# Experts with up to 232 tokens by four plain products, shorter switches on VectorE and ScalarE, and earlier gathers

## The chip, the cores and the metric

The kernel runs on one core of a Trainium2 chip. The metric is the device time of one launch in microseconds (us). Runs of one kernel differ by some tenths of a per cent.

## The reference, cut to what matters

A chunked attention (4 batches, 8 heads, 768 positions, heads of 64) makes 3072 rows of 512 numbers. A router then gives each row to one of eight experts, and each expert is a network of two layers without biases. All numbers are float32.

```python
logits = x @ w_gate                       # x: (3072, 512)
expert_idx = np.argmax(logits, axis=1)
...
for e in range(E):                        # E = 8, F = 1024
    lo, hi = (boundaries[e], boundaries[e + 1])
    h = np.maximum(x_sorted[lo:hi] @ w1[e], 0.0)     # w1[e]: (512, 1024)
    y_sorted[lo:hi] = h @ w2[e]                      # w2[e]: (1024, 512)
y = y_sorted[inv_perm]
return (gate_w[:, None] * y).astype(np.float32)
```

The inputs are random with a fixed seed. With them the eight experts receive 529, 195, 426, 381, 565, 320, 162 and 494 rows.

## The kernel before

**Attention and routing** fill the first 190 us or so. Each finished block of 96 rows is scattered to `x_dram` in the order of its experts. Of expert 0, 256 early rows are already done there by ordinary products (`early_rows`), so that 273 remain. `count_up` then counts the rows of each expert on VectorE, and works out `cases` (which variant of TensorE's code an expert takes) and `rows` (which rows of `x_dram` a gather fetches).

**The expert stage** is one critical section, written out by hand. `op` records a step: its engine, a function that emits it, and the tiles that it reads and writes. From these it works out the semaphore waits. The steps are collected in `plan`, and at the end `emit` writes them engine by engine; the order of recording is thus the order on each engine's queue, and nothing reorders it.

For each expert there is first an *interlude* (`interlude`): TensorE transposes the five gathered groups of 128 rows (`turn_x`; ScalarE copies groups 0, 2, 4 and VectorE 1, 3 into `xsT`), and then the five groups of the last expert's result (`turn_y`; VectorE scales group 1 into `y`, ScalarE the others). These transposes rotate over four halves of two PSUM tiles: `sum_x` (X) and `sum_q` (Q). VectorE also makes the first two differences T of the expert's rows.

Then comes the expert itself (`expert`), which is three calls of `layer`: the two halves of the first layer (k = 2 blocks of 128 in each quarter) and the last layer (k = 4). A call treats its matrix product as 2 x 2 quarters and does it by **seven products instead of eight**, with sums and differences of quarters (S of the weights, T of the rows), as in Strassen's method in Winograd's form. The expert's rows are split in two halves of up to 320 columns each, and the products work on one half's width. In the order of `layer` the products and what follows them on the other engines are:

1. P, then `over`: ScalarE copies P to R.
2. Q, then a snapshot of Q to a tile `kept`.
3. P again (added on top), then a snapshot of P.
4. R, then `evict(0, 0)`: ScalarE writes a quarter of the result.
5. P again, `over` once more, then `finish(1, 1)`: VectorE adds P and the first snapshot into a quarter of the result.
6. Q again, then `lift(1, 1)` (ScalarE's relu in the first layer) and `finish(0, 1)` on VectorE.
7. R again, then `lift(0, 1)` and `evict(1, 0)`.

The lists `at` place VectorE's sums S and T between these steps (`more(1)` to `more(7)`); among them are the sums S for the next expert's first layer, done during this expert's last layer. In the list the last of them stood at place 7, ahead of `finish(0, 1)`.

How many columns the products have is only known when the kernel runs. TensorE's code for an expert is therefore built in 24 **arms** (`ARMS`), one for each width of 136, 144 ... 320. A `Switch` on `cases` picks the arm; three products before an arm's end a hint is issued for the next expert's. VectorE and ScalarE have no switch: they always work on all 320 columns of a half.

```python
ARMS = list(range(136, HALF + 1, 8))
...
for a in nc.Switch(engines=[nc.tensor], index=[index[e]], n=len(ARMS), hint=f"expert{e}"):
    for i, s in enumerate(arm):
        if i == len(arm) - 3 and e + 1 < E:
            hint(e + 1)
        emit(s, ARMS[a])
```

**The queue of POOL** carries the stores of the results (`put`) and the gathers of the next expert's rows (`get_x`). Both are put in a list `sends`, and `tick` issues one of them after every second product of the first layer and after every product of the last; `pace` makes it wait until TensorE is there. `get_x` was called between the first layer and the last: a memset that marks all places of the row buffer as empty, and five gathers. The queue of SP carries the weights (`get_w`), after the first layer and after the last.

Of the kernel before, what the change touches and what calls it, by code (L numbers as in the profile page):

```python
# [73 lines left out]
ARMS = list(range(136, HALF + 1, 8))  # L74
# [430 lines left out]
def ordinary(ctx, tc, q, k, v, mem_k, mem_v, moe_w_gate, moe_w1, moe_w2, out, good):  # L505
# [352 lines left out]
    cases = cpool.tile([128, E], I32, name="cases")  # L858
    n0 = cpool.tile([128, 1], F32, name="n0")
# [34 lines left out]
    def count_up():  # L894
# [15 lines left out]
        nc.vector.tensor_copy(each, c)  # L910
        nc.vector.tensor_scalar(c, c, 7, None, op0=OP.add)
        nc.vector.tensor_scalar(c, c, 3, None, op0=OP.arith_shift_right)
        nc.vector.tensor_scalar(c, c, ARMS[0] // 8, HALF // 8, op0=OP.max, op1=OP.min)
        nc.vector.tensor_scalar(c, c, ARMS[0] // 8, None, op0=OP.subtract)
# [258 lines left out]
    def op(eng, fn, reads=(), writes=(), dma=None, where="after", pace=False):  # L1173
        need = {}

        def after(stamp):
            sem, n = stamp
            if not sem == eng == "PE" and known[eng].get(sem, 0) < n:
                need[sem] = max(need.get(sem, 0), n)

        if pace:
            after(("PE", counts["PE"]))
        for x in reads:
            if x in wrote:
                after(wrote[x])
        for x in writes:
            if x in wrote:
                after(wrote[x])
            for stamp in read.get(x, {}).items():
                after(stamp)  # L1190
        for sem, n in list(need.items()):
            if known[eng].get(sem, 0) >= n:
                continue
            for s, m in list(past.get((sem, n), {}).items()) + [(sem, n)]:
                known[eng][s] = max(known[eng].get(s, 0), m)
        sem, by = (dma, 16) if dma else (eng, 1)
        counts[sem] = counts.get(sem, 0) + by
        stamp = (sem, counts[sem])
        past[stamp] = dict(known[eng])
        for x in writes:  # L1200
            wrote[x] = stamp
            read[x] = {}
        for x in reads:
            read.setdefault(x, {})[sem] = counts[sem]
        plan.append((eng, fn, sorted(need.items()), (sem, by), where))

    def emit(step, n=None):
        eng, fn, need, (sem, by), _ = step
        first = []
# [75 lines left out]
    def get_x(e):  # L1285
# [3 lines left out]
        op("POOL", one_op(lambda: nc.gpsimd.memset(x[:, :, DM].bitcast(I32), SKIP)), [], [("xe", e % 2)])  # L1289
        for g in range(NG):  # L1290
# [11 lines left out]
            sends.append(lambda pace, g=g, fn=fn: batch(f"get{e % 2}", "POOL", fn, ("xe", e % 2), g == 0))  # L1302
# [54 lines left out]
    def product(to, names, A, B, reads, first, last, e, ms=(0, 1)):  # L1357
        k = A.shape[1]

        def fn(n):  # L1360
            made = []
            for m in ms:
                for i in range(k):
                    made.append(
                        mm(
                            to[:, m, 0:n],
                            lhsT=A[:, i, 128 * m : 128 * m + 128],
                            rhs=B[:, i, 0:n],
                            start=first and i == 0,
                            stop=last and i == k - 1,  # L1370
                            skip_group_check=True,
                        )
                    )
            return made[0], made[-1]
# [9 lines left out]
    def layer(e, A, a_names, S, s_names, B, b_names, T, t_names, C, c_names, relu, soon, at):  # L1384
# [17 lines left out]
        def evict(m, y, of, names):  # L1402
            op("ACT", one_op(lambda: nc.scalar.activation(C[m][y], of[:, :, 0:HALF], func)), [], names + [c_names[m][y]])
# [14 lines left out]
        product(P, p, A[0][0], B[0][0], [w] + b_names[0][0], True, False, e)  # L1418
# [4 lines left out]
        product(Q, q, S[0], T[0], [s_names[0], t_names[0]], True, False, e)  # L1423
        snapshot("M5", Q, q)
        more(5)
        product(P, p, S[1], T[1], [s_names[1], t_names[1]], False, False, e)
        snapshot("U2", P, p)
        more(6)
        product(R, r, A[0][1], B[1][0], [w] + b_names[1][0], False, True, e)
        evict(0, 0, R, r)  # L1430
        more(2)
        product(P, p, A[1][0], B[0][1], [a21] + b_names[0][1], False, True, e)
# [3 lines left out]
        product(Q, q, S[2], B[1][1], [s_names[2]] + b_names[1][1], False, True, e)  # L1436
# [14 lines left out]
        evict(1, 0, R, r)  # L1451
# [36 lines left out]
    def expert(e):  # L1488
        A1, A2 = quarters(e, 0), quarters(e, 1)
# [10 lines left out]
        for a in range(2):  # L1500
# [7 lines left out]
            layer(e, part, w1n, [x[:, :, a] for x in S1], s1n, B1, b1, T1, t1n, hs, hn, True, a == 1, at)  # L1508
        if e + 2 < E:
            get_w(e + 2, 0)  # L1510
        assert not sends
        if e < E - 1:
            get_x(e + 1)
            tick()
# [3 lines left out]
        at = {1: [t2[1]], 5: [t2[2], s2[3], s2[2]], 6: [t2[3]] + more[0:1], 2: more[1:2], 7: more[2:3]}  # L1518
        layer(e, A2, w2n, S2, s2n, B2, b2, T2, t2n, ys, yn, False, True, at)
# [6 lines left out]
    for e in range(E):  # L1526
# [3 lines left out]
        sums2[e] = weight_sums(e, 1, ["DVE"] * 4)  # L1530
    for g in range(2):
# [12 lines left out]
    with tc.tile_critical(no_gpsimd_drain=True):  # L1544
        for e in range(E + 1):
# [7 lines left out]
            for a in nc.Switch(engines=[nc.tensor], index=[index[e]], n=len(ARMS), hint=f"expert{e}"):  # L1553
                for i, s in enumerate(arm):
                    if i == len(arm) - 3 and e + 1 < E:
                        hint(e + 1)
                    emit(s, ARMS[a])
        for s in plan:
            if s[4] == "after":
                emit(s)  # L1560
# [50 lines left out]
```

## Time and profile before

| | |
|---|---|
| median of 3 runs | 538.32 us (535.3 to 539.24) |
| profiled execution | 532.34 us |
| its span, first to last instruction | 530.6 us |
| TensorE busy (PE) | 507.7 us, 96% of the span |
| TensorE's weight loads (PEld) | 475.7 us |
| VectorE (DVE) | 300.0 us, 57% |
| ScalarE (ACT) | 245.7 us, 46% |
| GpSimd (POOL) | 156.0 us, 29% |
| mean granted clock of TensorE | 0.994 |
| first transposes of expert 0 | at 190.46 us |
| first product of experts 1 to 7 | at 227.01, 258.49, 304.06, 345.14, 404.16, 439.32, 470.81 us |

The profile is of one execution, and all its times count from the first instruction. Busy time is the time in which an engine executes; an engine's sequencer, which handles loads of registers, jumps and hints, has rows of its own with a q (ACTq, DVEq, PEldq, POOLq, SPq). Lines such as L511 are those of the kernel before; L511 is the helper that every matmul goes through, L516 that of transposes, L1224 that of VectorE's sums, and L1227 that of ScalarE's copies `over` and `snapshot`, so groups are told apart by their tiles.

### The profile page before, as it was taken

To read this page: it belongs to the slowest core of one execution; us is meant where nothing else is said; L and a number is where in the kernel's file an instruction comes from. 1 tells how busy PE (TensorE), PEld (TensorE's weight loads), DVE (VectorE), ACT (ScalarE), POOL (GpSimd) and SP (SyncE) were. 2 spreads that over 40 slices of the span, in tenths; PEclk is the share of its full clock that TensorE was granted. 3 is DMA by queue.
4 is the path that set the end of the run, shared out by engine and by line. 5 is a ranking of instruction groups with operands and counts; after the bars stand their busy time and mean duration, and the time that the engine had idled before them with its cause. 6 is when DMAs were issued, how large, how long until landed. Compare 5 with 4: busy or idle time off the path is not lost.

```text
span 530.6 us, 9604 instructions
## 1 busy us (share of the span) xinstructions
PE 507.7 (96%) x3666; PEld 475.7 (90%) x3666; DVE 300.0 (57%) x565; ACT 245.7 (46%) x445; POOL 156.0 (29%) x186
## 2 busy tenths in 40 slices
PE   3999999999999989999999999999999999999992
PEld 3899999999998569999999999977779999999991
DVE  3455656566555246878656557443625767864611
ACT  2466656556632136374553454344216637454311
POOL 2000131323373604354135054121312434412003
PEclk9999999999999999999999999999999999999997
DMA  9999999989982302446406335330505334200002
GB/s 171 154 171 181 182 224 200 224 201 344 303 308 73 88 15 81 172 172 229 176 15 221 96 128 208 102 134 30 195 18 199 139 125 182 81 15 13 1 1 84
DMA packets 81350, 75.02 MB, mean 141 GB/s; under 512 B 39543, under 2 KB 64375, under 8 KB 81281
## 3 DMA queue, kind: packets, MB, share of 16 engines
q1 hardware_dynamic: 71840, 54.60, 41.6%
q0 software_dynamic: 8768, 19.29, 11.0%
q8 instruction: 46, 0.75, 0.6%
q10 hardware_dynamic: 672, 0.18, 0.1%
q14 instruction: 24, 0.19, 0.1%
HBM read 66.13 MB, written 17.50 MB: 158 GB/s over the span
## 4 chain that ended last, share of the span: by engine, by line
PE 83%; issue 9%; DMA 3%; POOL 2%; ACT 1%; DVE 1%; POOLq 0%; ACTq 0%
PE sum_p L511 20%; PE sum_r L511 13%; PE sum_q L511 13%; PE o L511 11%; PE sc L511 8%; PE tqk L516 4%; PE sum_x L516 3%; PE ph L511 3%; PE py L511 3%; PE sum_q L516 2%; PE tx L516 2%; POOL out_dram L1276 2%; DMA xe<-x_dram,rows 1%; DMA x_dram<-xr,dest 1%; DMA kn<-in_k_dram 1%
## 5 line engine op out<-in xcount | busy, mean ns | idle before, releaser
L1276 POOL DMA_INDIRECT out_dram<-y,xe x42 | 51.0, 1214 | 177.1 <-PE sum_q L511 59.9
L1293 POOL DMA_INDIRECT xe<-x_dram,rows x35 | 50.7, 1448 | 49.8 <-PE sum_r L511 29.2
L676 ACT ACTIVATE ex<-sc,cst 128x256 f32<-128x256 f32 x96 | 38.5, 472 | 56.5 <-PE sc L511 56.5
L511 PE MATMUL o<-v,ex 128*96 128x65 f32 x512 | 54.5, 251 | 0.0
L1227 ACT COPY sum_r<-sum_p 128x640 f32<-128x640 f32 x48 | 32.5, 677 | 47.3 <-PE sum_p L511 47.2
L511 PE MATMUL sc<-qT,kT 128*128 128x192 f32 x256 | 50.6, 343 | 1.1 <-ACT qT L627 1.1
L511 PEld LDWEIGHTS o<-v,ex 128*96 128x96 f32 x512 | 49.4, 167 | 0.0
L511 PE MATMUL sum_p<-xsT,w 128*128 128x136 f32 (+6 forms) x256 | 47.6, 329 | 0.5
L511 PE MATMUL sum_r<-t,w 128*128 128x136 f32 (+6 forms) x256 | 45.8, 326 | 0.0
L511 PE MATMUL sum_p<-t,s 128*128 128x136 f32 (+6 forms) x256 | 45.6, 326 | 0.0
L801 POOL DMA_INDIRECT x_dram<-xr,dest x32 | 30.2, 944 | 52.5 <-PE tqk L516 21.3
L511 PE MATMUL sum_q<-t,s 128*128 128x136 f32 (+6 forms) x256 | 45.1, 324 | 0.0
L511 PEld LDWEIGHTS sc<-qT,kT 128*128 128x128 f32 x256 | 43.2, 199 | 1.4 <-issue 1.4
L511 PEld LDWEIGHTS sum_p<-xsT,w 128*128 128x128 f32 x256 | 39.7, 190 | 4.8 <-issue 2.1
L511 PE MATMUL sum_p<-h,w 128*128 128x136 f32 (+6 forms) x256 | 43.8, 324 | 0.0
L511 PEld LDWEIGHTS sum_p<-t,s 128*128 128x128 f32 x256 | 39.7, 190 | 2.6
L511 PEld LDWEIGHTS sum_r<-t,w 128*128 128x128 f32 x256 | 39.6, 190 | 2.6
L511 PEld LDWEIGHTS sum_q<-t,s 128*128 128x128 f32 x256 | 39.8, 190 | 2.3
L511 PEld LDWEIGHTS sum_p<-h,w 128*128 128x128 f32 x256 | 39.5, 190 | 2.3
L1224 DVE TENSOR_TENSOR h<-sum_p,kept 128x640 f32<-128x640 f32 x16 | 13.2, 824 | 48.4 <-ACT sum_r L1227 48.4
L645 DVE COPY kT<-tqk 64x384 f32<-64x384 f32 x62 | 34.3, 554 | 10.4 <-PE tqk L516 9.8
L690 DVE RECIPROCAL inv_all<-o 96x4 f32<-96x4 f32 x64 | 11.4, 179 | 48.0 <-PE o L511 47.7
(154 smaller groups left out, 916.9 us busy)
## 6 DMA issues: line engine op xcount, KB each, us to landing
w<-in_moe_w_dram SPq DMA_DIRECT2D x14, 2048.0 KB, 8.6
kn<-in_k_dram SPq DMA_DIRECT2D x16, 384.0 KB
qn<-in_q_dram SPq DMA_DIRECT2D x16, 384.0 KB
w<-in_moe_w_dram SPq DMA_DIRECT2D x8, 512.0 KB
v<-in_v_dram SPq DMA_DIRECT2D x24, 128.0 KB
v<-in_v_dram SPq DMA_DIRECT2D x24, 112.0 KB
v<-in_v_dram SPq DMA_DIRECT2D x8, 144.0 KB
v<-in_v_dram SPq DMA_DIRECT2D x8, 96.0 KB
```

The lines of the kernel that those rows point to most:

```text
L511: i = nc.tensor.matmul(*args, **more)
L516: i = nc.tensor.transpose(*args)
L645: i = copy(to, of[:, :, 0:PAIRS].rearrange("d a (y z p) -> d a y z p", y=2, z=2))
L676: nc.scalar.activation(ex4[:, :, :, sl], sc4[:, :, :, sl], AF.Exp, bias=mask[:, 3 * x + g : 3 * x + g + 1], scale=D**-0.5)
L690: nc.vector.reciprocal(inv, o[:, :, D])
L801: i = nc.gpsimd.indirect_dma_start(out=x_dram, out_offset=bass.IndirectOffsetOnAxis(ap=dest[:, t : t + 1], axis=0), in_=xr[:, t % NXR].bit ...
L1224: op(eng, one_op(lambda: engines[eng].tensor_tensor(out, a, b, op=how)), reads, writes)
L1227: op("ACT", one_op(lambda: nc.scalar.copy(to, of)), reads, writes)
L1276: return nc.gpsimd.indirect_dma_start(out=out, out_offset=bass.IndirectOffsetOnAxis(ap=which.bitcast(I32), axis=0), in_=y, in_offset=None, ...
L1293: return nc.gpsimd.indirect_dma_start(out=x[:, g].bitcast(I32), out_offset=None, in_=x_dram, in_offset=bass.IndirectOffsetOnAxis(ap=rows[: ...
```

## The change

It has three parts.

- **A second way through an expert.** Thirteen arms are added (136 to 232 columns, marked True). They are taken where an expert has at most `FEW` = 232 rows. `count_up` then puts all rows in one half. In these arms a call of `layer` does the four plain products of its quarters: the first two product steps do one half of the lower quarter each into F (the tile P or Q), the step R does both upper products, and one of the steps 5 and 6 does the second lower product. The other steps, three in each call, are a single one-column matmul that keeps the semaphore counts (`nothing`). In the last layer, two matmuls of the R step cover 320 columns.
- **Switches on VectorE and ScalarE.** From an expert's start until a point in its last layer, each of their steps exists twice: as before, and as `few`, where it is a copy of one column (`skip`), or for `evict` a copy from the tile that now has the result. A `Switch` on `fews` picks one. ScalarE leaves it after the second snapshot of the last layer, VectorE after the last of that layer's T sums. The value is loaded and the hint given four steps before the next switch.
- **Gathers.** `get_x` for the next expert is called before the second half of the first layer rather than after the first layer; its memset is issued with the first gather.

Two smaller edits: the sum S that stood at place 7 of the last layer now stands at place 3, after `finish(0, 1)`; and two tiles `kept` are set to zero at the start of the critical section.

```diff
-ARMS = list(range(136, HALF + 1, 8))
+FEW = 232
+ARMS = [(n, False) for n in range(136, HALF + 1, 8)] + [(n, True) for n in range(136, FEW + 1, 8)]
...
         nc.vector.tensor_copy(each, c)
+        nc.vector.tensor_scalar(few, count, float(FEW), None, op0=OP.is_le)
+        nc.vector.tensor_tensor(more, count, each, op=OP.subtract)
+        nc.vector.tensor_tensor(more, more, few, op=OP.mult)
+        nc.vector.tensor_tensor(each, each, more, op=OP.add)
+        nc.vector.tensor_copy(c, each)
+        nc.vector.tensor_scalar(fews, count, float(FEW), None, op0=OP.is_le)
...
+    def skip(eng):
+        spot[0] = (spot[0] + 1) % 32
+        to = spots[eng][:, spot[0] : spot[0] + 1]
+        return one_op(lambda: skips[eng](to, cst[:, 0:1]))
+
+    inside = dict(DVE=None, ACT=None)
+
+    def op(eng, fn, reads=(), writes=(), dma=None, where="after", pace=False, few=None):
         need = {}
+        if inside.get(eng) is not None:
+            where = ("inside", inside[eng])
+            fn.few = few or skip(eng)
...
+        nothing = one_op(lambda: mm(unread, lhsT=ident[:, 0:1], rhs=ident[:, 0:1], start=False, stop=True, skip_group_check=True))
+        fn.few = of(few) if few else nothing
...
+        low0 = [[(F, A[1][0], B[0][0], True, False, [m], False)] for m in both]
+        low1 = [[], [(F, A[1][1], B[1][0], False, True, both, False)]][:: 1 if relu else -1]
+        up = [(R, A[0][0], B[0][0], True, False, both, not relu), (R, A[0][1], B[1][0], False, True, both, False)]
-        product(P, p, A[0][0], B[0][0], [w] + b_names[0][0], True, False, e)
+        product(P, p + fewer, A[0][0], B[0][0], [a21] + b0, True, False, e, few=low0[0])
...
         snapshot("U2", P, p)
+        if not relu:
+            inside["ACT"] = None
...
+            if a == 1 and e < E - 1:
+                get_x(e + 1)
...
-        if e < E - 1:
-            get_x(e + 1)
-            tick()
+        tick()
...
-        at = {1: [t2[1]], 5: [t2[2], s2[3], s2[2]], 6: [t2[3]] + more[0:1], 2: more[1:2], 7: more[2:3]}
+        end = [lambda: inside.update(DVE=None)]
+        at = {1: [t2[1]], 5: [t2[2], s2[3], s2[2]], 6: [t2[3]] + end + more[0:1], 2: more[1:2], 3: more[2:3]}
...
+                if i == ask and ask is not None:
+                    e = min(s[4][1] for s in steps[i:] if s[4] != "after")
+                    few = eng.value_load(fews[0:1, e : e + 1], min_val=0, max_val=1)
+                    nc.switch_hint(engines=[eng], index=[few], n=2, label=f"{name}{e}")
...
+                    for x in nc.Switch(engines=[eng], index=[few], n=2, hint=f"{name}{e}"):
+                        for t in body:
+                            emit(t, None, x == 1)
+                    ask = i + len(body) + len(rest) - 4 if e + 1 < E else None
```

## The prediction, made before the changed kernel ran

> **What bounds the kernel now.** I read the page first, then the windows of the experts, then the timelines of each engine at one expert's end and start, then the sequencers' rows by line.
>
> ```profile
> span 530.6 us, 9604 instructions
> PE 507.7 (96%) x3666; PEld 475.7 (90%) x3666; DVE 300.0 (57%) x565; ACT 245.7 (46%) x445; POOL 156.0 (29%) x186
> ...
> PE   3999999999999989999999999999999999999992
> ```
>
> PE is busy in every slice but the first and last. The windows run from one expert's first product to the next one's (PE busy comes second): nothing but PE sets the expert stage.
>
> ```profile
> core 0: us, PE busy (x) PEld busy (x) DVE busy (x) ACT busy (x) POOL busy (x), PEclk, DMA share, GB/s
> 227.01:258.49 31.48, 31.40 (x265) 30.74 (x265) 24.77 (x26) 19.07 (x30) 13.15 (x11) 1.00 0.52 183
> 345.14:404.16 59.02, 58.94 (x264) 46.91 (x265) 25.17 (x26) 19.40 (x30) 12.16 (x11) 1.00 0.28 98
> ```
>
> Experts 1 and 6 (227.01 and 439.32) run at the floor of 136 columns. The reference's routing with its seed gives them 195 and 162 tokens; expert 0's remainder is 273, all others have 320 or more. So these two alone take the new way, at 200 and 168 columns. PE's timeline (start, then busy) prices a column:
>
> ```profile
> 246.47 2.02 PE L511 MATMUL sum_r<-h,w 128*128 128x136 f32 x16
> 248.32 2.02 PE L511 MATMUL sum_p<-h,w 128*128 128x136 f32 x16
> ...
> 252.03 2.02 PE L511 MATMUL sum_r<-t,w 128*128 128x136 f32 x16
> 253.88 1.04 PE L516 MATMUL sum_x<-cst,xe 128*128 128x128 f32 x8
> ...
> 372.40 4.04 PE L511 MATMUL sum_p<-h,w 128*128 128x288 f32 x16
> 376.28 4.04 PE L511 MATMUL sum_q<-t,s 128*128 128x288 f32 x16
> ```
>
> From start to start 16 records take 1.85 us at 136 columns and 3.88 at 288: 115.7 and 242.5 ns each, so 0.834 ns a column and 2.3 besides. One matmul of the program is two records.
>
> **The change, part by part.** *Plain products.* An expert has 112 matmuls in 21 products; the few-way has 64 and nine one-column products. Expert 1 costs 128 records x 169.1 ns = 21.64 us, expert 6 128 x 142.4 = 18.23. Four records of the last layer's R product run 320 wide: 4 x 120 x 0.834 = 0.40 and 4 x 152 x 0.834 = 0.51. A one-column product is not in the trace; its bounds are 2.3+0.8 ns a record (the fit) and 115.7 (136 columns). The nearest row is the router's eight columns in the chain of waits:
>
> ```profile
> 160.99 0.95 PE o L511 x12
> ```
>
> 79 ns a record, so 18 records take 1.43 us (bounds 0.06 and 2.08). Arms: 23.47 and 20.17 us against 26.87 in both (253.88-227.01, 466.19-439.32). Gain 3.40 + 6.70 = **10.10 us**.
>
> *The end of a few-expert.* In the last layer ScalarE and VectorE have left their switches, so the copy P to R (677 ns) and two sums (0.82, next start 0.74 later) are really done, after product 5. Before, product 6 (1.85 us) covered them; now it has one column. Count from product 5's last start-to-start end. Its last record drains 0.16 later, ACT starts 0.04 after that and is done at 0.88; product 7, due at 0.16, starts at 0.93: 0.77 lost. Two transposed groups (0.435 each) end at 1.96; the third needs bank Q, which the second sum frees at 2.46: 0.55 lost. The weight sum s (1.13 to the next start) now stands behind it, so VectorE's copy of group 1 runs from 3.51 to 4.20; the first transpose of y needs its bank, due 3.82: 0.43 lost. VectorE then reads the switch's value (below, 1.3) before its next copy, 4.83 to 5.52; the third y transpose, due 5.12, waits 0.45. Sum 2.2, twice: **-4.4 us** (bounds: 0.77 each, product 7 alone; 3.5 each, if every later copy also waits its own 0.69 twice).
>
> *Reading and hinting the switch.* Each expert adds a load of `fews`, a hint and a jump on both engines, in front of the last four operations before the jump. On ScalarE these are the four copies of y. ScalarE's timeline and the sequencers' rows:
>
> ```profile
> 224.79 0.59 ACT L1246 COPY xsT<-sum_x 128x512 f32<-128x512 f32 x1 [0.29 <-PE sum_x L516]
> 225.27 0.70 ACT L1263 ACTIVATE y<-sum_x,xe 128x512 f32<-128x512 f32 x1
> 226.10 0.69 ACT L1263 ACTIVATE y<-sum_q,xe 128x512 f32<-128x512 f32 x1
> 226.69 1.26 ACT L1263 ACTIVATE y<-sum_x,xe 128x512 f32<-128x512 f32 x2
> 228.23 0.68 ACT L1227 COPY sum_r<-sum_p 128x640 f32<-128x640 f32 x1 [0.28 <-PE sum_p L511]
> ```
>
> ```profile
> L1137 SPq FUSED_REGOPS  x1: 181/181/181, 173.3 to 173.3; - x1
> L1137 ACTq TENSOR_LOAD <-good x1: 467/467/467, 181.9 to 181.9; - x1
> ...
> L1137 DVEq TENSOR_LOAD <-good x1: 542/542/542, 521.7 to 521.7; - x1
> ```
>
> SP's whole load of one value, check included, took 0.80 us (172.76 to 173.56); PE's hint took 0.54 (L1542, 214.34 to 214.88). Together 1.3. ScalarE's old load began 0.02 after the activation ahead of it had started, although that one had waited for PE: the sequencer did not run past a waiting instruction. So y of group 0 starts at 224.81+1.3 = 226.11 rather than 225.27 and ends at 226.80; the last transpose of y, due at 226.34, needs that bank and starts at 226.85: 0.5 us. VectorE's copy of group 3 goes from 224.35 to 224.8, done at 225.5 where 225.47 is due: nothing to speak of. Seven ends of experts have this; two are already in the sum above, so 5 x 0.5 = **-2.5 us** (bounds 0 and 0.8), and 0.15 at expert 0, whose first ScalarE copy at 191.15 comes just after the entry. [...]
>
> *The jump itself* takes PE 0.6 us (two moves, a sum, COMPARE_BRANCH 307 to 319 ns, a hint); on ScalarE it can run while the last two y copies (1.26 us) do, and the copy that follows still waits for product 1. I take nothing; without cover it is 0.6 us an expert where slack is smallest.
>
> *Costed at nothing.* Seven more small VectorE sums in `count_up`, 0.2 each: the rows would be ready at 173.4 rather than 172.03, the first gather starts at 179.18; uncovered 1.4. Two memsets of `kept` (2340 ns for 2640 elements, so 0.57 each) lie in POOL's idle time from 185.45 to 196.83. The update of the weights now also waits for product 2 (0.7 later, used by product 5: 0.6 left at 136 columns). The gathers: POOL now does five stores, the clearing memset, which waits for the stores to land, and five gathers within layers one and two of the same expert. Before, expert 1's last gather was issued at 248.76, median landing 4.3 us, needed at 253.88: 0.8 us to spare. A few-layer is 2.1 us shorter, so the old order would have been 1.3 late; the new one issues the last gather after the last layer's second product, some 9 us ahead. No cover is needed. SP's weight loads keep their place. First products now wait for the weights' second quarter too, which the same DMA brings. PE's hint still stands three products before an arm's end; in a few-expert 2.3 us of product 5 and the interlude's 4.6 follow it, where 10 did, and PE's jump is as before.
>
> Sum: 10.10 - 4.4 - 2.5 - 0.15 = **3.05 us** off. The profiled execution took 532.34 us (span 530.6, and 1.7 around it), so 529.3; the median shown is 538.32, 6.0 above it, and the same difference gives **535.3**.
>
> **Rivals.** *A, the ends are cheaper.* If the loads are hidden (2.5 and twice 0.45 back), the gain is 6.5 us: 531.8. For it: engines start the next copy before the last has ended. Against it: the load's row above.
>
> *B, jumps miss the code.* If the target's page must be fetched, an expert's first copy P to R comes later by D. The row of instruction packets in 186:193 shows what one is:
>
> ```profile
> q14 instruction: 2, 0.02, 1.0%
> ```
>
> 1.0% of 16 x 7 us over two packets is 0.56 us each. ScalarE is through with y 1.0 us after product 1 starts, the copy and its hand-over take 0.9, and product 3 is due after 16 records; so the slack is 1.0 at 216 columns, 0.7 at 192, 0.3 at 160, 1.45 at 248, 2.0 at 288 and about 0.1 in the few-experts, whose first two products are short. D = 1.0 costs 3.0 us and cancels the gain: from there it is slower. Two pages in a row, D = 2.2, cost 4.2 in the two, 1.2, 1.5, 1.9, 0.75 and 0.2 in the others and 0.5 at expert 0: 10.2, so 545.5. Against it: four engines jumped at 190.0 to 190.4 in these times, and those two packets are all that was fetched.
>
> ```profile
> L1606 ACTq COMPARE_BRANCH  x1: 38/38/38, 190.0 to 190.0; - x1
> L1606 DVEq COMPARE_BRANCH  x1: 53/53/53, 190.2 to 190.2; - x1
> ```
>  [...]
>
> *C, the few-way waits.* One-column products keep the full way's waits on ScalarE's and VectorE's stand-in copies (0.2 each). A round trip is some 0.25 us; I find it covered by neighbours of 0.57 us or more. If half of the 18 show 0.5, 4.5 us go: 539.8.
>
> **How the numbers follow.** Forecast 0.48 (its own range 533 to 537.5), A 0.22, B 0.18, C 0.12. This kernel's measurement tells about 1% (5.4 us). Faster takes A and a part of the forecast's lower edge, 0.26; slower takes B and half of C, 0.25; the rest is within. The bounds of the unknown costs put the gain between 11.3 us (10.10 + 2.74 - 1.54) and -2.4 (10.10 - 1.3 - 7.0 - 4.0 - 0.15), before B's jumps; the range of 529 to 543 leaves out the best of it and the worse half of B.
>
> **What would show it.** After: arms of experts 1 and 6 near 23.5 and 20.2 us; PE idle of 0.8 before their last product, on ACT; 0.5 idle before the last y transpose in each interlude, on ACT; ScalarE's TENSOR_LOAD beside 224.8; gathers done well before each interlude. Wrong if PE stands at an expert's first products (B), inside layer one of the two (C), or if the arms are not shorter.

## The result and the profile after

The changed kernel took **553.56 us** (median of 4; 550.79 to 558.15) against 537.18 for the kernel before in the same session: 1.031 times as long, 95% interval 1.023 to 1.040. It is slower by 16.4 us; the forecast was 535.3 and the range 529 to 543. Executions of one kernel lie up to 1.3% apart here, which is more than the tenths of a per cent said further up. The profiled execution took 553.05 us, its span is 551.2; the one of the kernel before (532.34) was shorter than all four timed ones, so the two profiles lie 20.6 us apart and the medians 16.4. First the page of the changed kernel, the lines that answer to those shown before:

```profile
span 551.2 us, 9545 instructions
PE 512.0 (93%) x3510; PEld 473.1 (86%) x3510; DVE 273.1 (50%) x572; ACT 230.5 (42%) x445; POOL 147.5 (27%) x188
...
PEclk9999999999979999979899999999999997999998
...
q14 instruction: 67, 0.55, 0.3%
```

The last two rows in the kernel before:

```profile
PEclk9999999999999999999999999999999999999997
...
q14 instruction: 24, 0.19, 0.1%
```

TensorE did 156 records fewer and was busy 4.3 us longer. The clock row has slices of 7 and 8 where the row before had 9 in all slices but the last. The queue q14 brought 67 packets of instructions; before it was 24. Then the windows from an expert's first product to the next one's, for experts 1, 4 and 6:

```profile
core 0: us, PE busy (x) PEld busy (x) DVE busy (x) ACT busy (x) POOL busy (x), PEclk, DMA share, GB/s
230.68:272.87 42.19, 32.78 (x186) 29.04 (x187) 11.36 (x27) 12.15 (x31) 10.52 (x11) 0.92 0.46 162
362.00:421.45 59.45, 59.13 (x265) 46.89 (x265) 25.22 (x26) 19.35 (x30) 12.84 (x11) 1.00 0.28 97
457.06:491.58 34.52, 28.84 (x186) 25.79 (x187) 10.14 (x26) 11.27 (x30) 10.60 (x11) 0.90 0.26 83
```

Expert 1, which was to become shorter, went from 31.48 to 42.19 us and expert 6 from 31.49 to 34.52. Expert 4, which takes the old way, lost 0.43. By first products the 20.8 us that the profiled execution lost up to its last matmul are: 3.2 ahead of expert 0, 0.5 in it, 10.7 in expert 1, 2.0 in expert 2, 0.4 to 0.5 in each of 3, 4 and 5, 3.0 in expert 6 and nothing in expert 7. The timeline at the start of expert 1 shows the largest piece:

```profile
230.06 1.27 ACT L1292 ACTIVATE y<-sum_x,xe 128x512 f32<-128x512 f32 x2
230.26 0.75 DVE L1294 TENSOR_SCALAR y<-sum_q,xe 128x512 f32<-128x512 f32 x1
...
230.68 1.61 PE L513 MATMUL sum_p<-xsT,w 128*128 128x200 f32 x8 [0.38 <-issue]
...
235.67 0.28 ACT L1192 COPY spots_ACT<-cst 128x1 f32<-128x1 f32 x2 [4.35 <-issue]
235.87 0.28 DVE L1192 COPY spots_DVE<-cst 128x1 f32<-128x1 f32 x3 [4.86 <-issue]
...
235.91 0.19 PE L513 MATMUL sum_p<-cst 128*1 128x1 f32 x2 [3.63 <-ACT spots_ACT L1192]
```

Both engines stop at their switch, for nothing but "issue", and TensorE's second step waits 3.63 us for ScalarE's stand-in copy. In the sequencers' rows ScalarE's COMPARE_BRANCH is at 230.52 and its next instruction at 235.59, **5.07 us** later; VectorE's are at 229.75 and 235.77, **6.03 us**. Two packets of q14 come at 233.12 and 233.14 and two at 236.2 and 236.4. At expert 6 it is 5.32 and 5.97, with TensorE idle for 4.14. Where the ordinary way is taken, the next instruction follows after 0.42 to 0.6. The row of the jump itself tells none of this; on these engines it is as short where they stop as where they don't:

```profile
L1635 ACTq COMPARE_BRANCH  x16: 37/43/61, 196.3 to 525.3; - x16
L1635 DVEq COMPARE_BRANCH  x16: 56/58/72, 197.9 to 522.1; - x16
```

TensorE's own jump stopped as well, ahead of expert 2; a jump of TensorE that stands for 1 us or more is called a miss from here on. The switch's rows before and after, and TensorE's idle time:

```profile
L1553 PEldq COMPARE_BRANCH  x16: 307/319/487, 192.2 to 515.7; - x16
```

```profile
L1616 PEldq COMPARE_BRANCH  x16: 300/314/3484, 195.4 to 536.5; - x16
```

```profile
272.87 2.16 PE L513 MATMUL sum_p<-xsT,w 128*128 128x216 f32 x5 [3.62 <-issue]
```

And in each of these three long stands, or as it ends, TensorE goes to half its clock. Windows of all four stretches at half clock before the kernel's end (the column behind POOL is the clock); the first, at 156, follows no stand above 0.9 us:

```profile
156.00:163.50 7.50, 7.47 (x39) 6.74 (x39) 2.23 (x14) 2.13 (x5) 4.80 (x7) 0.54 0.31 94
235.10:241.90 6.80, 5.99 (x21) 5.46 (x21) 0.28 (x3) 0.60 (x4) 1.01 (x1) 0.50 0.02 6
272.60:276.00 3.40, 3.13 (x9) 2.95 (x10) 0.00 (x0) 0.00 (x0) 0.00 (x0) 0.50 0.02 5
460.40:467.20 6.80, 4.60 (x18) 4.51 (x18) 0.28 (x3) 0.48 (x3) 0.00 (x0) 0.50 0.11 37
```

Half of the busy time in a stretch is lost: 3.0 us in expert 1, 1.6 in expert 2, 2.3 in expert 6. Expert 1's loss is thus 3.6 (switch) + 3.0 (clock) + 3.6 (TensorE's jump) and 1.1 for a stand among the transposes at 265.45, 11.3, less the 0.2 that the way itself gains (e10 below): 11.1 against the 10.7 measured. Expert 6 has 4.1 and 2.3 less a gain of 3.4: the 3.0 measured. The load of the switch, some 0.4 in each, is not in these two sums. The stretch at 156 lies in the attention; it goes with the 3.2 us ahead of expert 0. The attention's code is the same in all runs; ten of the eighteen below have such a stretch at 154 to 162, the kernels e6, e12 and e14 without the change among them, and eight have none. What brings it is open, and it isn't laid to the change.

### The profile page after: what moved, and what is told of

Its sections match the earlier page's. It is cut to its first block, busy times and chain, and to the rows that moved or that the text cites. A ratio compares the mean times of both kernels' runs of the same rounds, so it can differ in the third digit from the quotient of the medians.

```text
span 551.2 us, 9545 instructions
## 1 busy us (share of the span) xinstructions
PE 512.0 (93%) x3510; PEld 473.1 (86%) x3510; DVE 273.1 (50%) x572; ACT 230.5 (42%) x445; POOL 147.5 (27%) x188
## 4 chain that ended last, share of the span: by engine, by line
PE 81%; issue 12%; ACT 2%; POOL 2%; DMA 1%; DVE 0%; ACTq 0%; POOLq 0%; SPq 0%
PE sum_p L513 18%; PE sum_r L513 15%; PE o L513 12%; PE sum_q L513 11%; PE sc L513 8%; PE tqk L518 4%; PE sum_x L518 3%; PE ph L513 3%; PE py L513 2%; PE tx L518 2%; PE sum_q L518 2%; POOL out_dram L1305 2%; ACT y L1292 1%; DMA kn<-in_mem_k_dram 1%; ACT qT L629 0%
## 5 line engine op out<-in xcount | busy, mean ns | idle before, releaser
L513 PE MATMUL sum_p<-xsT,w 128*128 128x144 f32 (+7 forms) x224 | 45.9, 349 | 5.4 <-issue 5.3
L1325 POOL DMA_INDIRECT xe<-x_dram,rows x35 | 43.5, 1242 | 26.1 <-PE sum_p L513 8.0
L513 PE MATMUL sum_p<-h,w 128*128 128x144 f32 (+7 forms) x256 | 46.5, 335 | 0.1
L647 DVE COPY kT<-tqk 64x384 f32<-64x384 f32 x62 | 34.4, 554 | 10.7 <-PE tqk L518 10.0
L513 PE MATMUL sum_r<-t,w 128*128 128x144 f32 (+5 forms) x192 | 37.0, 340 | 0.0
L513 PE MATMUL sum_p<-t,s 128*128 128x144 f32 (+5 forms) x192 | 36.8, 340 | 0.0
L513 PE MATMUL sum_q<-t,s 128*128 128x144 f32 (+5 forms) x192 | 36.8, 340 | 0.0
L513 PE MATMUL sum_r<-xsT,w 128*128 128x200 f32 (+7 forms) x160 | 34.8, 373 | 0.0
L513 PEld LDWEIGHTS sum_q<-t,s 128*128 128x128 f32 x192 | 32.2, 191 | 2.3
L513 PEld LDWEIGHTS sum_p<-t,s 128*128 128x128 f32 x192 | 31.9, 190 | 2.4
L513 PEld LDWEIGHTS sum_r<-t,w 128*128 128x128 f32 x192 | 31.8, 190 | 2.3
```

Source lines behind the costliest of these rows:

```text
L513: i = nc.tensor.matmul(*args, **more)
L647: i = copy(to, of[:, :, 0:PAIRS].rearrange("d a (y z p) -> d a y z p", y=2, z=2))
L1325: return nc.gpsimd.indirect_dma_start(out=x[:, g].bitcast(I32), out_offset=None, in_=x_dram, in_offset=bass.IndirectOffsetOnAxis(ap=rows[: ...
```

## The experiments

All numbers stand beside runs of the kernel before on the same chip (medians 534.4 to 535.9 us). The first four kernels were run once each.

**e1: the hint earlier.** The value is loaded and the hint given right behind the last switch, 8 us ahead of the jump instead of 2.

```diff
-                    ask = i + len(body) + len(rest) - 4 if e + 1 < E else None
+                    ask = i + len(body) if e + 1 < E else None
```

> The changed kernel, but VectorE and ScalarE load the switch's value and give the hint right after they have left the switch before, not four steps before the next one. Theory 1, the hint comes too late: in the changed kernel the jump to the second way follows the hint by 1.7 us (ScalarE) and 2.1 us (VectorE) and the engine stands 5.1 and 6.0 us. With some 8 us more of lead the pause at experts 1 and 6 falls to 0.5 us or less, PE's idle time of 3.6 and 4.1 us there and the two stretches of half clock after them (6.8 us each, worth 3.4) go, and the loads no longer hold up the copies of y (0.45 in each of seven interludes): span 551.2 - 7.7 - 6.8 - 3.1 = 533.6, less if PE's own wait of 3.6 us before expert 2 goes too. Theory 2, every taken jump of these engines costs 5 us however early its hint: the pauses stay, only the 3.1 us go: 548.

548.26 us. The two entries still took 5.3 and 6.3 us at expert 1 (hints at 219.3 and 219.1, jumps at 227.75 and 227.16, packets only from 230.45 on). So 6 us more of lead did not help. The time fits "a taken jump always costs it", a theory that e11 then overturned: the number fitted and the reason was wrong.

**e2: no second way chosen.** Limit -1 in both comparisons with `FEW`; all 37 arms and the switches stay.

> The changed kernel with the limit of the second way set below zero, so that all switches are there and none takes the second way (experts 1 and 6 run as before the change). Both theories: no pause of 5 us and no half clock in the expert stage; the loads cost 0.45 us in each of seven interludes: span 530.6 + 3.1 = 533.7. If the event in the attention part of the changed kernel (1.1 us late and 6.8 us at half clock from 156.6 on, 3.3 us in all) belongs to the change, 537; if it comes by chance, it will be missing in some of these runs. If the leaving of the first way (a taken jump too) holds the engines up on PE's path, more than that.

542.5 us: no entry costs over 0.6, yet 6.6 us are lost where 3.1 were expected. TensorE still misses ahead of expert 2 (3.68 us). A leaving jump shows too, since the ordinary way ends in a jump over the other one; at 136 columns nothing covers it. The timeline at the end of expert 1:

```profile
252.56 0.70 ACT L1454 ACTIVATE yT<-sum_r 128x640 f32<-128x640 f32 x1 [3.93 <-issue]
253.35 0.68 ACT L1256 COPY sum_r<-sum_p 128x640 f32<-128x640 f32 x1
...
254.17 2.09 PE L513 MATMUL sum_r<-t,w 128*128 128x136 f32 x16 [1.36 <-ACT sum_r L1256]
```

ScalarE idles 3.93 us at "issue", and TensorE waits 1.36 for its copy.

**e3: the ways exchanged.** The second way is put first, so that the ordinary one is jumped to.

```diff
-        nc.vector.tensor_scalar(fews, count, float(FEW), None, op0=OP.is_le)
+        nc.vector.tensor_scalar(fews, count, float(FEW), None, op0=OP.is_gt)
...
-                            emit(t, None, x == 1)
+                            emit(t, None, x == 0)
```

> The changed kernel with the two ways of VectorE's and ScalarE's switches in the other order: the second way lies first (no jump into it), and the ordinary way is jumped to, so that six experts jump instead of two. Theories 1 and 2 both say that the pause is the jump's: it goes from experts 1 and 6 (7.7 us of idle time and 6.8 of half clock back) and comes to the six others, where products 1 and 2 cover a part of it: 2.8 us at 216 columns, 3.1 at 192, 1.8 at 288, 3.5 at 160, 2.4 at 248 and some 3 at expert 0, 16.6 in all, and up to 3.4 for the half clock after each: 553 to 573. Rival, the steps of the second way themselves are slow: 551 as before, with the idle time still in experts 1 and 6.

548.39 us, under what either theory gave: long products cover much of the jump (TensorE is busy for 2.4 to 4.1 us in the three longest windows below). Now experts 1 and 6 enter in 0.42 to 0.51 us, and the six others pay. Windows from ScalarE's jump to its next instruction, at experts 0, 2, 3, 4, 5 and 7 (length first, DMA share second from the end):

```profile
193.04:195.81 2.77, 2.77 (x19) 2.59 (x19) 1.72 (x3) 0.40 (x1) 0.00 (x0) 1.00 0.05 12
260.54:264.01 3.47, 0.09 (x1) 0.10 (x1) 0.47 (x1) 0.80 (x2) 0.00 (x0) 1.00 0.42 152
311.52:316.28 4.76, 2.86 (x16) 2.57 (x16) 0.47 (x1) 0.80 (x2) 1.03 (x1) 1.00 0.77 289
355.95:360.95 5.00, 4.14 (x16) 2.96 (x16) 0.55 (x2) 0.79 (x2) 0.49 (x1) 1.00 0.59 226
417.25:422.64 5.39, 2.43 (x16) 2.20 (x16) 0.47 (x1) 0.79 (x2) 1.03 (x1) 1.00 0.71 260
486.47:489.45 2.98, 2.98 (x14) 2.73 (x15) 1.12 (x2) 0.78 (x2) 0.78 (x1) 1.00 0.05 14
```

The jump's cost belongs to the place of the way, not to its content. ScalarE's took 2.8 to 3.0 us at a DMA share of 0.05, 3.5 at 0.42, and 4.8 to 5.4 at 0.59 to 0.77, while weights were landing.

**e4: e1 with the gathers at their old place.**

> As e1_ask_early, but the gathers are again called after the first layer, as before the change. By the prediction's sum the last gather is then issued about when product 4 of the last layer ends in a few-expert, lands 4.3 us later, and is 1.3 us or more late for experts 2 and 7: 2.6 to 5 us slower than e1_ask_early, as PE idle before the first transposes on the gather's DMA. Rival, the gathers' place does not matter: the same time as e1_ask_early.

560.82 us, 12.6 more than e1. TensorE missed at the jumps out of both second-way arms (3.4 us at 262.3, 3.6 at 487.6), which e1 did not, beside the miss into expert 2 that both have; the mean clock was 0.956 where e1's was 0.980. The run doesn't answer its question; e16 does.

**e5: no switches on VectorE and ScalarE**, the second way written straight into their streams.

```diff
-                    for x in nc.Switch(engines=[eng], index=[few], n=2, hint=f"{name}{e}"):
-                        for t in body:
-                            emit(t, None, x == 1)
+                    for t in body:
+                        emit(t, None, s[4][1] in (1, 6))
```

> The switches of VectorE and ScalarE are taken out, with their loads and hints: the stand-in copies of experts 1 and 6 are written straight into their streams, so the choice of these two experts is fixed in the program and not read from the counts; TensorE keeps its 37 arms. Theory (the taken jumps on the two engines, 5.1 to 6.3 us each, are what stops TensorE): against the changed kernel's 553 us, the two stalls (3.6 and 4.1) go, with the half clock after them (2 x 3.4), the load and the hint of each interlude (7 x 0.45 = 3.1), so 536 to 533; the arms of experts 1 and 6 are then near 23.5 and 20.2 us plus 1 to 2 of the end, and the missed jump of TensorE ahead of expert 2 (3.5 + 1.7) stays. Rival (the one-column products and the stand-in copies wait for each other, whatever the jumps do): the stalls at the first products of experts 1 and 6 stay and the time is above 545.

538.93 us (ratio 1.005, 1.0005 to 1.009). The stalls at the first products are gone, the rival falls; TensorE's misses are 4.2 us at the entry of expert 2 and 3.4 at the jump out of expert 6; the second was not foreseen, and the time lies above the 533 to 536 that were expected.

**e6 and e12: the kernel before with more arms that are never chosen**, 37 and 32.

```diff
-ARMS = list(range(136, HALF + 1, 8))
+ARMS = list(range(136, HALF + 1, 8)) + list(range(136, 233, 8))
```

> The kernel before with 13 more arms of TensorE (136 to 232 columns once more, never chosen), nothing else. Theory (with 37 arms instead of 24 the jump into expert 2 leaves what was fetched): a compare-and-branch of some 3.5 us ahead of expert 2, 1.7 us of half clock after it, 541 us against 536. Rival (TensorE's miss comes from instruction fetches of VectorE and ScalarE, or from their new code): no such miss, 536 us.

> The kernel before with 8 more arms of TensorE, 32 in all, never chosen. It stands beside 24 arms (534.8, no miss) and 37 (555.2, four misses inside the expert stage). Theory (more arms, more misses: what counts is how far the arms reach): one to four misses, 540 to 555. Rival (it is where the arms come to lie, and 32 like 24 is a multiple of 8): no miss, 535.

555.15 us (1.041, 1.034 to 1.049) and 559.7 us (1.047, 1.039 to 1.055). This was the surprise: code that never runs costs the kernel before as much as the whole change. Rows of TensorE's switch with 37 and with 32 arms, and the timeline of the first at expert 1:

```profile
L1553 PEldq COMPARE_BRANCH  x16: 297/399/4368, 194.7 to 538.3; - x16
```

```profile
L1553 PEldq COMPARE_BRANCH  x16: 302/403/5233, 193.4 to 537.4; - x16
```

```profile
233.14 1.18 PE L511 MATMUL sum_p<-xsT,w 128*128 128x136 f32 x8 [3.44 <-issue]
```

With 37 arms the entries of experts 1, 2, 4 and 6 took 3.66, 4.37, 2.44 and 3.64 us; with 32 those of 1, 2, 3, 4 and 6 took 3.86, 5.23, 1.38, 2.52 and 3.97. I had expected one miss. Being a multiple of 8 doesn't help 32.

**e7: 24 arms and no second way chosen.** As e2, without the 13 arms.

> The changed kernel with the second way never chosen (limit -1 in place of 232) and TensorE's 13 arms for it left out: VectorE and ScalarE keep their switches, loads and hints, and always fall into the ordinary way. It stands beside the run with the second way never chosen and 37 arms, 542.5 us. Theory (the 13 arms cause TensorE's miss): no miss, 3.7 + 1.7 us less, 537 us; what is then left over the kernel before is the load and hint of 7 interludes (2.5 to 3) less 0 and 1.4 us at expert 1, where both engines leave the switch by a jump. Rival (the code or the fetches of the two engines cause it): the miss stays, 542.

536.09 us (1.004, 1.0006 to 1.0074), with no miss of TensorE in the expert stage: the theory's 537. What is left of the loss are the loads and the leaving jump (TensorE idle for 0.90 us at 251.0).

**e8: TensorE kept busy during the stall**, by 28 matmuls into unread columns in each of the 13 arms.

> The changed kernel, where TensorE does 28 matmuls of 128 columns into unread columns (some 3 us) behind the first product of each expert's second way, while it would stand there for the two engines' jumps. Theory (TensorE's clock is halved for 6.83 us because it stood for 3.6 to 4.1 us): it no longer stands, the clock stays, 2 x 3.4 us less: 546 us against 553. Rival (the halving has another cause, such as the many short matmuls): 553 or more, with the same half-clock stretches at experts 1 and 6.

586.42 us. It tells nothing of the clock: the longer arms made TensorE miss at six of the seven entries of experts 1 to 7, by 2.8 to 6.0 us. Like e6, it shows that an edit of TensorE's code moves its misses, also between arms that were not edited.

**e9: the change with 24 arms.**

```diff
-ARMS = [(n, False) for n in range(136, HALF + 1, 8)] + [(n, True) for n in range(136, FEW + 1, 8)]
+ARMS = [(n, False) for n in range(144, 289, 8)] + [(n, True) for n in range(168, 201, 8)]
...
-        lowest, halves = ARMS[0][0] // 8, HALF // 8 - ARMS[0][0] // 8 + 1
+        lowest, halves = ARMS[0][0] // 8, 16
```

> The changed kernel with 24 arms of TensorE in place of 37: 144 to 288 columns for the ordinary way (19 arms), 168 to 200 for the second (5); what these leave out (other counts) this input never asks for, and its eight experts take the same widths as in the changed kernel. VectorE and ScalarE keep switches, loads and hints. Theory (TensorE misses its code because the table has 37 arms; the two engines miss theirs because their jump is taken): no compare-and-branch of TensorE above 1 us inside the expert stage, the jumps of VectorE and ScalarE at experts 1 and 6 still 5 to 6 us: 553 less 3.5 and 1.7 (expert 2), 547 to 548. Rival (the number of arms is not it): the miss into expert 2 stays, 553.

538.7 us (1.007, 1.003 to 1.010): 14.9 less than the changed kernel where 5 to 6 were expected. No jump of TensorE missed inside the expert stage:

```profile
L1616 PEldq COMPARE_BRANCH  x16: 304/312/487, 196.4 to 528.3; - x16
```

VectorE and ScalarE still took 4.4 to 5.4 us at experts 1 and 6, but TensorE stood 2.96 and 3.49 instead of 3.63 and 4.14, and the half clock after it lasted 3.41 instead of 6.83 both times. That and the miss with its half clock make up some 8.5 of the 14.9; the rest isn't placed, as the profiled execution (545.0) was this kernel's longest.

**e10: 24 arms and no switches on the two engines.**

> The 24 arms of the run before together with no switches on VectorE and ScalarE: experts 1 and 6 are fixed as the two of the second way in the program of these two engines. Theory (the products' saving of 10.1 us is real and only code fetches ate it): 534.8 for the kernel before, less 10.1, plus 3 to 4.4 for the ends of the two experts: 528 to 529, with no missed jump. Rival (the second way itself is not shorter by as much): 533 or more.

531.75 us (0.994, 0.990 to 0.998): faster than the kernel before, and half of what the theory gave. This is the second way without any miss. TensorE's timeline at expert 1:

```profile
239.02 0.19 PE L513 MATMUL sum_r<-cst 128*1 128x1 f32 x2
239.14 2.98 PE L513 MATMUL sum_p<-h,w 128*128 128x200 f32 x16
242.04 0.19 PE L513 MATMUL sum_p<-cst 128*1 128x1 f32 x2
...
250.88 0.19 PE L513 MATMUL sum_q<-cst 128*1 128x1 f32 x2
251.81 0.19 PE L513 MATMUL sum_r<-cst 128*1 128x1 f32 x2 [0.74 <-ACT sum_r L1256]
252.31 1.09 PE L518 MATMUL sum_x<-cst,xe 128*128 128x128 f32 x8 [0.32 <-issue]
```

A one-column product takes 0.12 us from start to start, and a wide product between two of them 0.2 longer than its records (2.90 for 16, where 16 x 169.1 ns is 2.71): its first record takes 0.10 more and its last 0.09. That makes 0.31 a step. Expert 1 took 31.24 us instead of 31.48, expert 6 28.05 instead of 31.49: 3.7 us in all.

**e11: the hint inside the arm.** The value is loaded one expert ahead, and VectorE's and ScalarE's hint stands three steps before their arm's end.

```diff
+                        for j, t in enumerate(body):
+                            if j == len(body) - 3 and e + 1 < E:
+                                nc.switch_hint(engines=[eng], index=[then], n=2, label=f"{name}{e + 1}")
+                            emit(t, None, x == 1)
```

> The 24 arms, and the hint of VectorE's and ScalarE's next switch given inside the arm, two operations before its end, as TensorE's is; the value is loaded one expert ahead. Theory 1 (on these two engines a taken jump fetches its page after the jump, whatever was hinted): entries of experts 1 and 6 still take 5 to 6 us, 547 to 548 as with the 24 arms alone. Theory 2 (a hint works where it is given inside the arm, as it does on TensorE): an instruction packet follows the hint by 2 us, the two entries take 0.5 us, the stalls of 3.6 and 4.1 and the half clock after them go: 533.

533.35 us (0.998, 0.994 to 1.001). The entries and the time are those of theory 2. Its sign in the packets did not come: the inner hints for expert 1 are at 208.31 and 209.27, and the next packets of q14 come at 215.34 to 218.48, behind the jumps out of the arm (211.75 and 213.67), four as in the changed kernel. At the entry there are two where the changed kernel has four. The hints also stand 16 to 18 us ahead of the jump where e1's stood 8, so place and lead were varied together. That these entries no longer stop is shown; by what is not. The timeline at expert 1 again:

```profile
225.59 1.26 ACT L1292 ACTIVATE y<-sum_x,xe 128x512 f32<-128x512 f32 x2
225.92 0.74 DVE L1294 TENSOR_SCALAR y<-sum_q,xe 128x512 f32<-128x512 f32 x1
...
225.93 1.73 PE L513 MATMUL sum_p<-xsT,w 128*128 128x200 f32 x8
226.58 0.14 DVE L1192 COPY spots_DVE<-cst 128x1 f32<-128x1 f32 x1
...
226.91 0.19 ACT L1192 COPY spots_ACT<-cst 128x1 f32<-128x1 f32 x1
...
227.59 0.19 PE L513 MATMUL sum_p<-cst 128*1 128x1 f32 x2
```

The stand-in copies follow the last y at once, and TensorE doesn't wait. The entries took 0.42 and 0.54 us at expert 1, 0.41 and 0.51 at 6. One miss is left to TensorE, 3.49 us at the jump out of expert 6; e16 has it too (3.76). The expectations of e13 and e18 take it for the jump into expert 7, and that of e17 takes e13's miss, out of expert 1, for one into expert 2. The load, now ahead of the switch, is also hidden: expert 4 took 59.16 us, where it was 59.02 before and 59.45 in the changed kernel.

**e15: the same hints with 37 arms.**

> The changed kernel with its 37 arms, VectorE's and ScalarE's hints given inside the arm. Theory (the two causes add up): the two entries take 0.5 us instead of 5 to 6, so 553.6 less 3.6 + 4.1 and less up to 6.8 of half clock: 539 to 546; TensorE's miss into expert 2 stays. Rival (the inner hints helped only with 24 arms): 550 or more, entries at 5 us.

539.71 us (1.006, 1.002 to 1.010), 13.9 less than the changed kernel. TensorE's miss into expert 2 is still there (4.2 us). So either remedy alone gives 14 to 15 us and both give 20.2: the gains overlap, they don't add, and why is not shown. The runs are of different sessions, in which the kernel before had medians of 534.4 to 537.2.

**e16: e11 with the gathers at their old place.**

> The run with 24 arms and inner hints (533.4), with the gathers put back to their old place, behind the products of layer two, as in the kernel before. Theory (the prediction's: a second-way expert is so short that the old place is 1.3 us or more late): TensorE waits for gathered rows ahead of the transposes of experts 1 and 6, 1.3 to 4 us each, with half clock where it is over 2.7: 536 to 543. Rival (the gathers' place is worth nothing): 533 to 534.

533.44 us (0.992, 0.989 to 0.996), within the noise the same as e11 (0.998, 0.994 to 1.001): no worth of the earlier gathers can be seen. The last gather of expert 2's rows, on POOL, and the transposes that need them:

```profile
249.78 1.00 POOL L1325 DMA_INDIRECT xe<-x_dram,rows  x1 [3.50 <-PE sum_r L513]
...
253.57 1.09 PE L518 MATMUL sum_x<-cst,xe 128*128 128x128 f32 x8 [0.31 <-issue]
...
255.49 0.60 PE L518 MATMUL sum_x<-cst,xe 128*128 128x128 f32 x4
```

The group that this gather brings is read last, at 255.5, 5.7 us after its issue, without a wait.

**e14: TensorE's hint behind the leaving jump** (kernel before, 37 arms).

```diff
-                    if i == len(arm) - 3 and e + 1 < E:
-                        hint(e + 1)
...
+            if 0 < e < E:
+                hint(e)
```

> The kernel before with 37 arms, where TensorE's hint of the next expert stands behind the jump out of the arm, at the head of the interlude, some 5.5 us ahead of the next jump, and not three products ahead of the arm's end. Theory 1 (with 37 arms the hinted page is fetched and then pushed out by the jump that leaves the arm): the page now comes last and stays, no misses, 535 to 537 against 555. Theory 2 (a hint holds only where it is given inside the arm, as on VectorE and ScalarE): all seven jumps miss by 3.5 us or more, half clock after most, 565 to 580.

544.95 us (1.015, 1.010 to 1.020). Both theories fall: the misses at experts 1 and 6 go, those at 2 and 4 stay (the longest jump takes 3.35 us).

**e13, e17 and e18: a kernel for every count, and the outer hint with 24 arms.** e13 is e11 with 12 ordinary arms in steps of 16 columns and 12 of the second way in steps of 8; e17 is e13, and e18 is e16, with TensorE's hint as in e14.

> Hints inside the arms, and 24 arms that serve every count: the ordinary way in steps of 16 columns from 144 to 320 (12 arms), the second in steps of 8 from 144 to 232 (12). This input's experts 2 and 7 then run at 224 and 256 columns in place of 216 and 248: 224 records x 8 x 0.834 ns = 1.5 us each, 3 in all. Theory (all that counts is the number of arms and the place of the hint): 533.4 + 3 = 536.4 if the run beside it had its missed jump into expert 7 (3.5 + 1.7) in most executions, 531 to 532 if that miss goes; so 531 to 537. Rival (which arm lies where decides the misses, not their number): new misses, above 540.

> The 24 arms that serve every count, inner hints on VectorE and ScalarE, and TensorE's hint behind the jump out of its arm, at the head of the interlude. Theory (the page that the inner hint of TensorE fetched is pushed out by the leaving jump): the miss into expert 2 (3.7 and 1.7 of half clock) goes: 537.9 - 5.4 = 532.5, faster than the kernel before. Rival (a short expert's interlude leaves too little time, or something else loses the page): the miss stays or moves to another expert, 537 to 540.

> The run with 24 arms for this input, inner hints and late gathers (533.4), with TensorE's hint behind the jump out of its arm. Theory: the miss into expert 7 (3.8 and 1.7 of half clock) goes: 528. Rival: the miss stays or moves, 533 or more.

537.86 us (1.004, 1.001 to 1.008), 556.01 (1.039, 1.035 to 1.042) and 556.32 (1.036, 1.034 to 1.039). e13 has one miss, at the jump out of expert 1 (3.69 us), and doesn't beat the kernel before. With the hint outside, 24 arms miss at experts 1, 2, 4, 6 and 7 (e18 at 3 too, 1.0 us), and the longest jump takes 4.83 and 4.63 us: what helped 37 arms ruins 24. So the number of arms decides through something else that these runs don't show. Not settled is which jump of TensorE misses and why: in all these traces a packet of 16384 bytes follows each hint, mostly within 3 us, also where the jump then misses; in the changed kernel it starts 1.4 us behind the hint for expert 2, whose jump took 3.48. Pushed out, fetched from the wrong place, or forgotten: the traces can't tell.

Of the versions run, e10 and e16 beat both kernels, by under 1% against the kernel before; e16 decides from the counts, but serves only the widths that this input needs.

## Why the prediction was wrong

**The step that failed** is "*The jump itself* ... I take nothing". It was priced on TensorE's row, whose jumps are hinted inside the arm, and on two jumps at 190 that did not stop. That reading could not show the cost: on ScalarE and VectorE the jump's row is 0.04 and 0.06 us long even where the engine then stops for 5 to 6. The trace before had a jump that did stop, TensorE's over the general program behind the expert stage (3.74 us), and it was not weighed:

```profile
L1579 PEldq COMPARE_BRANCH  x1: 3741/3741/3741, 521.3 to 521.3; - x1
```

In the changed kernel the taken jump cost VectorE and ScalarE 5.1 to 6.0 us, of which TensorE stood 3.6 and 4.1. Rival B named such a stop, by a fetch of code, with the right place (no slack in the few-experts), yet its D came from a packet's own 0.56 us. Not the packet is long (0.31 and 0.36 in q14's rows at expert 1) but the time around it: it comes 2.6 us after ScalarE's jump, and the next instruction 2.1 us after its end. B also charged all eight experts, where only the two that took the jump stopped. The entry jumps, over 15 steps (VectorE) and 19 (ScalarE), stalled by 2.8 (e3) to 6.3 us (e1) every time they were taken without a hint inside the arm that was left; that they are short did not spare them.

**"PE's jump is as before"** failed too: the 13 arms were counted as free because they aren't executed. e6, e7, e9 and e12 show that they are not; in the changed kernel TensorE's jump into expert 2 took 3.48 us.

**No term for the clock.** In the expert stages of all traces TensorE stood 42 times for more than 2.7 us, and with 41 of these stands came half clock, in stretches of 3.41 us or a multiple (3.41 and 6.83 in the changed kernel); of the 15 from 0.9 to 2.6 us two had it (2.25 and 2.37 us, in e4 and e14). A stand did not have to be over for it: the one at 458.46 in the changed kernel, 4.14 us long, had lasted 1.9 us when the clock fell. The prediction should have asked of any stall it considered whether half clock comes with it.

**Terms that were mis-sized.** *Plain products, 10.10 us.* In e10 the arms, without the waits at their end, are 25.03 and 21.85 us against the predicted 23.47 and 20.17: 6.9 us gained. The one-column steps are the reason: nine at 0.31 are 2.8 us, outside the bounds of 0.06 and 2.08. What was left out is the 0.2 that a wide product takes longer between two short ones, in its first and its last record. *The ends, -4.4 us.* In e10 the wait ahead of product 7 is 0.74 (predicted 0.77), 0.3 follow, and the interlude is 0.55 longer: 1.6 an expert, 3.2 in all. Together a gain of 3.7 was there to be had, not 5.7.

**Right.** The bound, the two experts and their widths; the loads, 0.43 to 0.47 us in each of experts 3 to 5 where 0.5 was predicted; nothing for `count_up` and the memsets (e10's first product of expert 0 is 0.8 us earlier than before). The gathers' nothing was right and its reason wrong: the old order is not 1.3 us late (e16).

**Rivals.** A's cheaper ends came in part and C's waits did not appear in e10; B came nearest: the taken jumps stopped, with packets of q14 inside the stop, at the place that it named for the two few-experts; its 545.5 holds 6.0 us for the six other experts, which did not pay, and nothing for TensorE's miss and the clock.

## What to carry to other kernels

A jump is priced on its own engine and by its hint: look in the rows for what an unhinted or wrongly hinted jump costs there (here 2.8 to 3.0 us on ScalarE at a DMA share of 0.05 and 4.8 to 5.4 at 0.59 to 0.77 in e3, and up to 6.3 on VectorE in e1), and look at the next instruction, since the jump's own row can hide the stop. On these two engines, give the hint inside the arm that is left (the entries then took 0.41 to 0.54 us, e11). Variants that are never chosen are not free (13 more arms cost 4.1%, 8 more 4.7%); run the old kernel with nothing but the added code before building on it. Of TensorE's stalls above 2.7 us, 41 of 42 came with half clock: count it on top, in the changed kernel 1.6 to 3.0 us each.

## What was not expected of the hardware

Eight arms of code that no expert takes made a kernel 4.7% slower (e12, 3.9 to 5.5%). Hints on VectorE and ScalarE shortened no taken entry when given outside an arm, even 8 us ahead (5.3 and 6.3 us, e1); with hints inside one, 16 us or more ahead, the entries took 0.41 to 0.54 us (e11). With TensorE's hint outside the arm, the jumps into two of the experts 1 to 7 missed with 37 arms (e14), and into five and six of them with 24 (e17, e18). A jump of ScalarE took 2.8 us at a DMA share of 0.05 and 5.4 at 0.71 (e3).
